# Which engine copies which PSUM tile, and in which PSUM unit a group lands: a spectral filter mix on one core

## The chip, the cores and the metric

The kernel runs on one core of a Trainium2 chip. A core has five engines that run their own instruction streams and meet at semaphores: TensorE (PE in the profile; its weight loads have a row of their own, PEld), VectorE (DVE), ScalarE (ACT), GpSimd (POOL) and SyncE (SP, used here to issue transfers). TensorE writes its results to PSUM, 8 banks of 512 float32 per partition; DVE and ACT copy them from there to SBUF. The metric is device time of the one core in microseconds, the median of several executions.

## The reference

Two global spectral filters, A and B, are applied to the same input `x` of 2048 by 1024 (bfloat16), and a gate per row mixes their results:

```python
X = rfft2(x)                       # over rows (2048) and columns (1024)
a = irfft2(X * (A_w_r + 1j * A_w_i))
b = irfft2(X * (B_w_r + 1j * B_w_i))
g = sigmoid((x * gate_w).sum(-1))  # one value per row
out = g * a + (1 - g) * b
```

The weights are 2048 by 513 each. `B_x` is not used.

## The kernel before, in words

There is no FFT instruction, so each Fourier transform is a chain of matrix products with constant tables. The 2048 rows are split as 32 times 64. The stages, in order:

- **Stage 1** (`stage1`): the 32-point transform along the rows, after DVE has folded the columns of `x` into sums and differences (`fold`).
- **Stage 2** (`stage2(i)`, 16 steps): the transform along the columns, two blocks of rows per step. 16 matmuls (L451, L460) write two banks: 0 and 1 for even `i`, 6 and 7 for odd. One copy, here called CS`i` (L466), brings the 128x1024 result to one of three buffers `CS` in SBUF, in bfloat16 and reordered.
- **Stage 4** (`stage4(i)`, 16 steps): the 64-point transform along the rows. Its matmuls (L477) read CS`i` and write banks 2 and 3 for even `i`, 3 and 4 for odd `i`, and banks 0 and 1 in the last step, 15. Bank 3, which two neighbouring steps share, is written by the second half of a step's matmuls. One copy, called X`i` (L485 on DVE or L487 on ACT), brings the result to one of eight buffers `X`. `swap(i)` then issues two transfers (L283) that exchange real and imaginary rows of X`i` into one of seven buffers `XS`; POOL's queue issues them up to step 8 and SP's queue from step 9 on.
- **Products** (`product`, L508, all on DVE): the spectrum, plain ("A") or swapped ("B"), times part 0 or 1 of both filters' weights. Results replace the weights in SBUF.
- **Stage 5** (`group`): the inverse 64-point transform, 32 groups of 8 columns each. A group is 16 matmuls (`group_mm`, L604) into one PSUM unit, a pair of banks (unit u is banks 2u and 2u+1), and one copy (`group_out`, L613 on DVE or L615 on ACT) out of it.
- **Stage 6** and **stage 7**: the inverse 32-point transform, in which the gate is mixed in through 16 tables (`rbgen`, L593, DVE), then the inverse transform along the columns and the final sums (L793, L829 on DVE, L834 on POOL) and stores.
- Beside these the row gate is computed from the spectrum: `gate_spectrum` (L522) after stage 2, `star_column` and `col0` for column 256, and `zsum` (L563, with the sigmoid copies L566) in stage 5.

The order of the work on each engine is the order of the calls to `P.add`; there is no planner. A dependence becomes a wait on a semaphore that counts the finished instructions of the other engine. Every engine works in its order, so an instruction that waits holds everything behind it. Around the change that order is:

- Steps 0 to 13 run `step(i)`: stage 4 of step i, X`i`, the swap, then stage 2 of step i+2 and CS`i+2`; after it gate sums, products from the list `ORDER[i]`, and in the first steps `save512` and the folds `fold3` that stage 2 will read later. So ACT copies X0, CS2, then CS3, X2, CS4, then CS5, X4, CS6, and so on; X1 and X3 are on DVE, in front of the products of their step.
- At the start of stage 5 a list `slots` says which unit comes next: `spare()` takes its first entry and puts it at the end. It begins as 3, 2, 1; unit 0 holds stage 4's step 15. Group 1 goes to unit 3, X15 is copied, group 2 goes to unit 2, the star column (a 32-wide result) to unit 1. Then unit 0 is put into the list at its end (L703): the order from there on is 3, 2, 1, 0. The groups that follow, 3, 4, 5, 6 and so on, take the units in this rotation. A group waits until the copy out of its unit is done.
- Groups run in the order 1 to 15, 0, then 16 to 31. All copies of groups are on ACT, but groups 20 and 27 (n of 4 and 11 in the loop at L722) and group 30 are on DVE. The 16 `rbgen` are issued on DVE right behind group 20's copy. Groups 30 and 31 are interleaved in two halves (`last_groups`).
- Stage 6 of row block 0 uses the unit that the rotation gives it by an assertion at L732; stage 7 uses fixed banks, `b0`, that alternate with the parity of r.

Of the kernel before, what the change touches and what calls it, by code (L numbers as in the profile page):

```python
# [5 lines left out]
ACT = mybir.ActivationFunctionType  # L6
# [226 lines left out]
def bass_gated_mix__spectral_gfnet__spectral_gfnet__prompt_kernel(nc, A_x, A_w_r, A_w_i, B_x, B_w_r, B_w_i, gate_w, out):  # L233
# [24 lines left out]
    def sl(t, off, dims, p0=0, np_=128, pstep=1):  # L258
        n = t.shape[1]
        return AP(t, p0 * n + off, [[n * pstep, np_]] + [list(x) for x in dims])  # L260

    def ps(col, dims):
        return AP(PS, col, [[4096, 128]] + [list(x) for x in dims])

    def bank(b):
        return ("ps", b)

    def fbo(kind, pm, m):
        return 128 * (4 * kind + 2 * pm + m)
# [6 lines left out]
    P = Prog()  # L276
# [18 lines left out]
    for _ in range(18):  # L295
        P.add("pe", lambda e: e.matmul(ps(7 * 512, [(1, 256)]), sl(CL, GRo, [(1, 128)]), sl(CL, GRo, [(1, 256)]), start=True, stop=True),
              r=["GRz"], w=[bank(7)])
# [124 lines left out]
    def fblock(cmb, j, t):  # L422
        if cmb in (1, 2):
            return sl(FT, cmb * 4096 + j * 2048 + t * 128, [(1, 128)])
        if t < 4:
            return sl(W, Eo(t // 2, cmb // 3, j) + t % 2 * RP, [(1, 128)])
        return sl(FT, cmb * 4096 + j * 2048 + (t - 4) * 128, [(1, 128)])

    def ekeys(i, cs, s):
        return [("E", i, cs, s)]  # L430
# [11 lines left out]
    def stage2(i, css=(0, 1), ab=(0, 1)):  # L442
        hf, p = SEQ[i]
        b0 = 6 * (i % 2)
        if 0 in ab:
            for cs in css:
                for t in (2 * p, 2 * p + 1):
                    for j in range(2):
                        o = ps((b0 + t % 2) * 512 + cs * 256 + 32, [(96, 2), (64, 2), (1, 32)])
                        rh = sl(F2, 256 + 512 * cs + 256 * j + hf * 128, [(1, 128)])  # L450
                        P.add("pe", lambda e, o=o, cs=cs, j=j, t=t, rh=rh: e.matmul(o, fblock(1 + cs, j, t), rh, start=(j == 0), stop=(j == 1)),  # L451
                              r=[("F1a" if p < 2 else "F1", cs, j), "F2"], w=[bank(b0 + t % 2)])
        if 1 in ab:
            for cs in css:
                for t in (2 * p, 2 * p + 1):
                    for w in range(2):
                        v = 1 - w if cs else w
                        o = ps((b0 + t % 2) * 512 + cs * 256 + 64 * v, [(224 - 128 * v, 2), (1, 32)])
                        rh = sl(F2, 1280 * cs + w * 128 + hf * 64, [(1, 64)])
                        op = P.add("pe", lambda e, o=o, cs=cs, t=t, w=w, rh=rh: e.matmul(o, fblock(3 * cs, w, t), rh, start=True, stop=True),  # L460
                                   r=ekeys(p, cs, w) + ["F2"], w=[bank(b0 + t % 2)])
        if css == (0,) or ab == (0,):
            return
        dst, src = sl(XF, CSo(i), [(1, 1024)]), ps(b0 * 512, [(128, 8), (1, 32), (32, 4)])
        kw = dict(r=[bank(b0), bank(b0 + 1)], w=[("CS", i % 3)], after=last1)
        P.add("act", lambda e: e.activation(dst, src, ACT.Copy), **kw)  # L466
        return op

    def stage4(i):
        bk = ((2, 3), (3, 4))[i % 2] if i < 15 else (0, 1)  # L470
        parts = [(1, 0, 1), (0, 1, 1)] if SEQ[i][1] == 0 else [(0, 0, 2)]
        for pm in (1, 0) if bk[0] == 3 else (0, 1):
            for kind, q, n in parts:
                for m in range(2):
                    o = ps(bk[pm] * 512 + q * 256, [(1, n * 256)])
                    rh = sl(XF, CSo(i) + 512 * q + 256 * m, [(512, n), (1, 256)])
                    P.add("pe", lambda e, o=o, kind=kind, pm=pm, m=m, rh=rh: e.matmul(o, sl(CK, fbo(kind, pm, m), [(1, 128)]), rh,  # L477
                                                                                      start=(m == 0), stop=(m == 1)),
                          r=[("CS", i % 3), "CK"], w=[bank(bk[pm])])

        def out():
            dst, src = sl(XF, Xo(i), [(1, 1024)]), ps(bk[0] * 512, [(256, 2), (512, 2), (1, 256)])
            kw = dict(r=[bank(k) for k in bk], w=[("X", Xk(i))], after=last1)
            if i in (1, 3):
                P.add("dve", lambda e: e.tensor_copy(dst, src), **kw)  # L485
            else:
                P.add("act", lambda e: e.activation(dst, src, ACT.Copy), **kw)  # L487

        return out

# [126 lines left out]
    def group(u, g, eng):  # L617
        group_mm(u, g, range(8), lambda q: q)
        group_out(u, g, eng, 0, 8, 1, 0, [("Z", 0), ("Z", 1)])
# [60 lines left out]
    slots = [3, 2, 1]  # L680

    def spare():
        slots.append(slots.pop(0))
        return slots[-1]
# [3 lines left out]
    def groups(n):  # L688
        for _ in range(n):
            group(spare(), todo.pop(0), "act")  # L690
# [9 lines left out]
    groups(1)  # L700
    star_column(2 * spare())
    dma("sp", "U5", sl(FT, U5o, [(2048, 8), (1, 1024)]).bitcast(u16), cst["U5"].ap().rearrange("p (a b) -> p a b", a=8), w=["U5"], after=[last2])
    slots.insert(3, 0)  # L703
    groups(8)
    for a in rest(10):
        product(*a)
# [15 lines left out]
    for n, g in enumerate(range(16, 32)):  # L722
        if n == 14:
            last_groups([spare(), spare()])
        elif n < 14:
            group(spare(), g, "dve" if n in (4, 11) else "act")
        if n == 1:
            zsum([spare(), spare()])
        if n == 4:
            for _ in range(16):  # L730
                rbgen(rb.pop(0), "dve")
    assert slots[-2:] == [0, 3], slots  # L732
    last5 = P.ops["pe"][-1]


# [1 line left out]
    Yo = lambda k, r: (8 * k + r // 2) * RP + 264 + r % 2 * 128  # L737
    OUT = [(MM, 1024 * k) for k in range(4)] + [(XF, 6144 + 1024 * k) for k in range(2)]

    S6B = lambda r: 4 if r % 2 else 6 if r else 2  # L740

    def stage6_mm(r, bs, pis):
        b0 = S6B(r)
        t6, o6, _ = RBS[r]
# [11 lines left out]
    def stage6(r):  # L756
        b0 = S6B(r)
        for k in range(2 if r == 0 else 1):
# [12 lines left out]
    def stage7(r):  # L771
        nonlocal pqc
        full, half = r in FULL, r in HALF
        b0 = 34 - 2 * r if r >= 14 else 2 * (r % 2)
        ot, oo = OUT[r % NOU]
        eo = 4096 + r % 2 * 1024
        es = sl(XF, eo, [(1, 1024)]).bitcast(f32)
# [20 lines left out]
        if full:  # L798
            for k in range(4):
                mm((b0 + 1) * 512, 0, 2, 1, k // 2, k % 2, k, 3)  # L800
            even(0, 512)
            for k0, n, bk in ((0, 2, b0),) if r < 15 else ((0, 1, b0), (1, 1, 0)):
                for k in range(4):
                    mm(bk * 512, k0, n, 0, k // 2, k % 2, k, 3)
                finals(k0, n, bk, XF, eo, [("EO", r % 2)])
        elif half:
            for e_ in (1, 0):
                for k in range(2):
                    mm((b0 + 1) * 512 + e_ * 256, 0, 1, 1, k, k ^ e_, k, 1)
            even(256, 256)  # L810
            for k in range(4):
                mm(b0 * 512, 0, 2, 0, k // 2, k % 2, k, 3)
            to = 4096 + (r % 2) * 1024
            for s, op in enumerate((ALU.add, ALU.subtract)):
                P.add("dve", lambda e, s=s, op=op: e.tensor_tensor(out=sl(MM, to + s * 512, [(1, 512)]).bitcast(f32),
                                                                   in0=ps((b0 + 1) * 512, [(1, 256)]), in1=es[:, :256], op=op),
                      r=[("EO", r % 2), bank(b0 + 1)], w=[("T", r % 2, s), ("XS", 4), ("XS", 5)])
            finals(0, 2, b0, MM, to, [("T", r % 2, 0), ("T", r % 2, 1)])
        else:
            for e_ in (1, 0):  # L820
                for ri in range(2):
                    for k in range(2):
                        mm((b0 + e_) * 512 + ri * 256, 0, 1, ri, k, k ^ e_, k, 1)
            even(0, 512)
            pk = pqc % NPQ
            pqc += 1
            pq = pk * 4096
            for s, op in enumerate((ALU.add, ALU.subtract)):
                P.add("dve", lambda e, s=s, op=op: e.tensor_tensor(out=sl(FT, pq + s * 2048, [(1, 1024)]).bitcast(f32), in0=ps(b0 * 512, [(1, 512)]),  # L829
                                                                   in1=es, op=op),  # L830
                      r=[("EO", r % 2), bank(b0)], w=[("PQ", pk, s)], after=[last5])
            pv = sl(FT, pq, [(2048, 2), (1, 1024)]).bitcast(f32).rearrange("p a (b c) -> p a b c", b=2)
            for s, op in enumerate((ALU.add, ALU.subtract)):
                P.add("pool", lambda e, s=s, op=op: e.tensor_tensor(out=ods(s, 0, 2), in0=pv[:, :, 0, :], in1=pv[:, :, 1, :], op=op),  # L834
                      r=[("PQ", pk, 0), ("PQ", pk, 1)], w=[("OU", r % NOU, s, k) for k in range(2)])
# [91 lines left out]
```

## Time and profile before

| | us |
|---|---|
| median of 3 runs | 119.57 (119.42 to 119.87) |
| the profiled execution | 119.76 |
| its span, first to last instruction | 117.6 |
| PE busy in the span | 110.5 |
| DVE busy | 101.4 |
| ACT busy | 97.5 |
| POOL busy | 33.8 |
| mean granted TensorE clock | 1.000 of full speed |

How to read it: all times inside the profile count from the span's first instruction; the 2.2 us between span and execution time lie around it. A row of the timeline gives the start, the duration, the engine, the source line (L485 is line 485 of the kernel), the operation, what it writes and reads, and, in brackets, how long its engine had been idle and what ended the idle time. Neighbouring instructions of one kind are merged into one row (x16). A row of the list of waits reads: engine, line, what it waited for, microseconds in total, how many times, the longest. The stages lie about here in the span: stage 1 up to 20.7, stages 2 and 4 from 20.8 to 51, stage 5 from 50.8 to 85.4, stages 6 and 7 from 85.3 to the end.

### The profile page before, as it was taken

The numbers are of one execution on the slowest core, as the hardware profiler recorded it, in microseconds if no ns is written. First come the engines' busy times: TensorE is split into PE (matmuls) and PEld (weight loads), VectorE is DVE, ScalarE is ACT, GpSimd is POOL, SyncE is SP. The second block draws the span as 40 slices with busy tenths as digits, with TensorE's granted clock in tenths as the row PEclk, the third lists the DMA queues.
The fourth block names the chain that finished last, engine by engine and source line by source line (L and its number), as shares of the span: only waits on it lengthen the run. The fifth ranks groups of instructions, "written<-read, shape, count | busy, mean of one in ns | idle before, by whom it ended". The sixth has DMA issues, their size and how long they took to land.

```text
span 117.6 us, 4242 instructions
## 1 busy us (share of the span) xinstructions
PE 110.5 (94%) x1812; PEld 88.5 (75%) x1812; DVE 101.4 (86%) x210; ACT 97.5 (83%) x117; POOL 33.8 (29%) x43
## 2 busy tenths in 40 slices
PE   6999999999999999997999999999989999999960
PEld 4566898875766757686999999999978777777530
DVE  0468998989999999999999999699569999899980
ACT  5239998988799999959999999997977889998620
POOL 1000030016655600000000000000003999999920
PEclk9999999999999999999999999999999999999999
DMA  3999999999999999963399800000000134426465
GB/s 72 303 416 417 416 358 353 354 347 351 370 361 359 368 363 363 361 230 137 84 342 398 298 6 0 6 0 6 0 6 3 66 147 155 178 95 224 154 243 188
DMA packets 17682, 26.14 MB, mean 222 GB/s; under 512 B 2112, under 2 KB 11072, under 8 KB 17664
## 3 DMA queue, kind: packets, MB, share of 16 engines
q1 hardware_dynamic: 16368, 23.00, 55.5%
q0 software_dynamic: 864, 2.36, 5.6%
q10 hardware_dynamic: 432, 0.52, 1.6%
q8 instruction: 14, 0.23, 0.8%
q14 instruction: 4, 0.03, 0.1%
HBM read 17.48 MB, written 4.19 MB: 184 GB/s over the span
## 4 chain that ended last, share of the span: by engine, by line
PE 79%; DMA 6%; ACT 4%; DVE 4%; SPq 2%; issue 2%; DVEq 0%
PE PS L604 25%; PE PS L782 15%; PE PS L477 12%; PE PS L379 9%; PE PS L753 6%; DMA W<-in_A_x_dram 6%; PE PS L451 6%; PE PS L460 3%; PE PS L522 2%; SPq L283 2%; ACT XF L487 2%; ACT W L615 1%; DVE XF L485 1%; DVE MM L793 1%; ACT XF L789 1%
## 5 line engine op out<-in xcount | busy, mean ns | idle before, releaser
L604 PE MATMUL PS<-CL,W 128*128 128x128 bf16 x512 | 32.2, 224 | 0.7 <-ACT W L615 0.6
L604 PEld LDWEIGHTS PS<-CL,W 128*128 128x128 bf16 x512 | 31.7, 145 | 1.1 <-ACT W L615 0.8
L834 POOL TENSOR_TENSOR MM<-FT 128x512 bf16<-128x512 f32 x14 | 17.5, 1297 | 48.9 <-DVE FT L829 48.9
L615 ACT ACTIVATE W<-PS 128x1024 bf16<-128x1024 f32 (+1 forms) x30 | 29.1, 1009 | 2.7 <-PE PS L604 2.6
L508 DVE TENSOR_TENSOR W<-XF,W 128x1024 bf16<-128x1024 bf16 (+1 forms) x38 | 22.4, 608 | 0.8 <-ACT XF L487 0.5
L508 DVE TENSOR_TENSOR W<-MM,W 128x1024 bf16<-128x1024 bf16 (+1 forms) x38 | 22.4, 613 | 0.4 <-DMA MM<-XF 0.2
L782 PE MATMUL PS<-FT,W 128*128 128x256 bf16 (+1 forms) x132 | 19.6, 299 | 0.2
L477 PE MATMUL PS<-XF,CK 128*128 128x512 bf16 (+1 forms) x72 | 17.9, 357 | 0.2 <-DVE XF L485 0.2
L766 ACT ACTIVATE W<-PS 128x1024 bf16<-128x1024 f32 (+1 forms) x15 | 14.8, 992 | 3.9 <-PE PS L753 3.9
L466 ACT ACTIVATE XF<-PS 128x1024 bf16<-128x1024 f32 x16 | 17.0, 1072 | 1.1 <-PE PS L460 1.0
L340 DVE TENSOR_TENSOR XF<-W 128x512 bf16<-128x512 bf16 (+2 forms) x34 | 11.4, 403 | 6.0 <-DMA W<-in_A_x_dram 5.8
L782 PEld LDWEIGHTS PS<-FT,W 128*128 128x128 bf16 x132 | 12.0, 98 | 5.4 <-DVE XF L793 0.7
L487 ACT ACTIVATE XF<-PS 128x1024 bf16<-128x1024 f32 x14 | 15.2, 1085 | 0.6 <-PE PS L477 0.6
L379 PE MATMUL PS<-MM,XF 128*128 128x256 bf16 x128 | 15.2, 276 | 0.5 <-DVE XF L340 0.3
L379 PEld LDWEIGHTS PS<-MM,XF 128*128 128x128 bf16 x128 | 12.3, 99 | 3.5 <-DVE XF L340 1.8
L390 ACT ACTIVATE FT<-PS 128x1024 bf16<-128x1024 f32 (+2 forms) x15 | 13.1, 1012 | 0.8 <-PE PS L379 0.8
L283 POOL DMA_DIRECT2D MM<-XF x18 | 9.9, 551 | 13.6 <-PE PS L477 8.0
L829 DVE TENSOR_TENSOR FT<-PS,XF 128x512 f32<-128x512 f32 x18 | 11.5, 684 | 0.5 <-ACT XF L789 0.2
L451 PEld LDWEIGHTS PS<-F,FT 128*128 128x128 bf16 x128 | 8.4, 98 | 3.1 <-ACT FT L390 0.2
L451 PE MATMUL PS<-F,FT 128*128 128x128 bf16 x128 | 10.2, 219 | 0.0
L789 ACT ACTIVATE XF<-PS 128x512 f32<-128x512 f32 (+1 forms) x16 | 8.5, 533 | 1.4 <-PE PS L782 1.4
L477 PEld LDWEIGHTS PS<-XF,CK 128*128 128x128 bf16 x72 | 4.7, 97 | 6.3 <-ACT XF L487 4.7
(62 smaller groups left out, 104.5 us busy)
## 6 DMA issues: line engine op xcount, KB each, us to landing
W<-in_A_x_dram SPq DMA_DIRECT2D x7, 512.0 KB, 7.5
out_dram<-MM SPq DMA_DIRECT2D x10, 256.0 KB, 2.3
MM<-XF POOLq DMA_DIRECT2D x18, 128.0 KB, 5.3
FT<-c_U SPq DMA_DIRECT2D x1, 2048.0 KB, 9.6
MM<-XF SPq DMA_DIRECT2D x14, 128.0 KB, 2.7
W<-in_A_w_r_dram SPq DMA_DIRECT2D x4, 256.5 KB, 6.4
W<-in_A_w_i_dram SPq DMA_DIRECT2D x4, 256.5 KB, 6.6
W<-in_B_w_r_dram SPq DMA_DIRECT2D x4, 256.5 KB, 6.9
```

Source lines behind the costliest of these rows:

```text
L379: P.add("pe", lambda e, o=o, lh=lh, rh=rh, s=s: e.matmul(o, lh, rh, start=(s == 0), stop=(s == 1)), r=[("xf", c % 2, q, h, s ^ j), ("M", c ...
L390: P.add("act", lambda e, s=src, d=dst: e.activation(d, s, ACT.Copy), **kw)
L451: P.add("pe", lambda e, o=o, cs=cs, j=j, t=t, rh=rh: e.matmul(o, fblock(1 + cs, j, t), rh, start=(j == 0), stop=(j == 1)), r=[("F1a" if p ...
L466: P.add("act", lambda e: e.activation(dst, src, ACT.Copy), **kw)
L477: P.add("pe", lambda e, o=o, kind=kind, pm=pm, m=m, rh=rh: e.matmul(o, sl(CK, fbo(kind, pm, m), [(1, 128)]), rh, start=(m == 0), stop=(m = ...
L487: P.add("act", lambda e: e.activation(dst, src, ACT.Copy), **kw)
L508: P.add("dve", lambda e: e.tensor_tensor(out=rows((1 - h) * 64 * RP + sw * HW), in0=sl(xt, xo + 128 * h + 64 * h0, [(0, 2), (256, 4 * ni), ...
L604: P.add("pe", lambda e, o=o, l0=l0, ab=ab: e.matmul(o, sl(W, HW * ab + l0, [(RP, 128)]), sl(CL, KIo[ab], [(1, 128)]), start=(ab == 0), sto ...
L615: P.add("act", lambda e: e.activation(dst, src, ACT.Copy), r=b, a=keys)
L766: P.add("act", lambda e, s=src, d=dst: e.activation(d, s, ACT.Copy), **kw)
L782: P.add("pe", lambda e: e.matmul(ps(col, [(1, n * 256)]), lh, rh, start=(k == 0), stop=(k == last)), r=[("Y", r), "DI"] + ["DJ"] * (full o ...
L834: P.add("pool", lambda e, s=s, op=op: e.tensor_tensor(out=ods(s, 0, 2), in0=pv[:, :, 0, :], in1=pv[:, :, 1, :], op=op), r=[("PQ", pk, 0), ...
```

## The change

Four edits, all of them on the order and placement of work; what is computed stays the same.

1. In stage 2 the copies CS3 and CS5 go from ACT to DVE; in stage 4 the copies X1 and X3 go from DVE to ACT.
2. Unit 0 is put into the rotation behind unit 3 in place of the end: the order becomes 3, 0, 2, 1. Group 4, the fourth of stage 5, lands in the unit that stage 4's step 15 used, group 5 in unit 2, group 6 in unit 1.
3. Group 19 is copied by DVE and group 20 by ACT (before, the other way round), and the 16 `rbgen` follow group 19's copy.
4. As the rotation ends differently, stage 6's row block 0 uses banks 0 and 1 (before 2 and 3), and stage 7's banks for even and odd r change places.

```diff
@@ stage2
-        P.add("act", lambda e: e.activation(dst, src, ACT.Copy), **kw)
+        if i in (3, 5):
+            P.add("dve", lambda e: e.tensor_copy(dst, src), **kw)
+        else:
+            P.add("act", lambda e: e.activation(dst, src, ACT.Copy), **kw)
@@ stage4
-            if i in (1, 3):
-                P.add("dve", lambda e: e.tensor_copy(dst, src), **kw)
-            else:
-                P.add("act", lambda e: e.activation(dst, src, ACT.Copy), **kw)
+            P.add("act", lambda e: e.activation(dst, src, ACT.Copy), **kw)
@@ start of stage 5
-    slots.insert(3, 0)
+    assert slots == [3, 2, 1]
+    slots.insert(1, 0)
     groups(8)
@@ second half of stage 5
-            group(spare(), g, "dve" if n in (4, 11) else "act")
+            group(spare(), g, "dve" if n in (3, 11) else "act")
         if n == 1:
             zsum([spare(), spare()])
-        if n == 4:
+        if n == 3:
             for _ in range(16):
                 rbgen(rb.pop(0), "dve")
-    assert slots[-2:] == [0, 3], slots
+    assert slots[-2:] == [1, 3], slots
@@ stage 6 and stage 7
-    S6B = lambda r: 4 if r % 2 else 6 if r else 2
+    S6B = lambda r: 4 if r % 2 else 6 * (r > 0)
...
-        b0 = 34 - 2 * r if r >= 14 else 2 * (r % 2)
+        b0 = 34 - 2 * r if r >= 14 else 2 - 2 * (r % 2)
...
-            for k0, n, bk in ((0, 2, b0),) if r < 15 else ((0, 1, b0), (1, 1, 0)):
+            for k0, n, bk in ((0, 2, b0),) if r < 15 else ((0, 1, b0), (1, 1, 2)):
```

## The prediction, made before the changed kernel was run

> **What bounds the kernel now.** I read the busy line and the chain of the page first, then the list of waits, then the timeline of the two places that the change touches. From the page and the list of waits:
>
> ```profile
> PE 110.5 (94%) x1812; PEld 88.5 (75%) x1812; DVE 101.4 (86%) x210; ACT 97.5 (83%) x117; POOL 33.8 (29%) x43
> PE 79%; DMA 6%; ACT 4%; DVE 4%; SPq 2%; issue 2%; DVEq 0%
> ...
> PEld PS L477 <- ACT XF L487: 4.7, 12, 0.5
> PEld PS L477 <- DVE XF L485: 1.2, 2, 0.7
> PEld PS L604 <- ACT W L615: 0.8, 1, 0.8
> ```
>
> PE carries 79% of the chain, so what counts is where PE stands still. In stages 2 to 4 it waits at L477 (stage 4's second pair of matmuls) for the copy of the step before, because two neighbouring steps share bank 3: 12 times behind ACT, twice behind DVE. In stage 5 the list holds one wait worth having, 0.8 us. Now the first steps of stage 4 (start, duration, engine, line; in brackets the idle time before and who ended it):
>
> ```profile
> 25.19 1.02 ACT L466 ACTIVATE XF<-PS 128x1024 bf16<-128x1024 f32 x1
> 26.00 1.23 DVE L485 CAST XF<-PS 128x1024 bf16<-128x1024 f32 x1
> 26.71 1.02 ACT L466 ACTIVATE XF<-PS 128x1024 bf16<-128x1024 f32 x1 [0.50 <-PE PS L460]
> 27.27 0.11 PEld L477 LDWEIGHTS PS<-XF,CK 128*128 128x128 bf16 x2 [0.70 <-DVE XF L485]
> 27.92 1.02 ACT L487 ACTIVATE XF<-PS 128x1024 bf16<-128x1024 f32 x1 [0.18 <-PE PS L477]
> 28.84 1.02 ACT L466 ACTIVATE XF<-PS 128x1024 bf16<-128x1024 f32 x1
> 29.65 1.22 DVE L485 CAST XF<-PS 128x1024 bf16<-128x1024 f32 x1
> 30.36 1.02 ACT L466 ACTIVATE XF<-PS 128x1024 bf16<-128x1024 f32 x1 [0.51 <-PE PS L460]
> 30.92 0.11 PEld L477 LDWEIGHTS PS<-XF,CK 128*128 128x128 bf16 x2 [0.50 <-DVE XF L485]
> 31.57 1.02 ACT L487 ACTIVATE XF<-PS 128x1024 bf16<-128x1024 f32 x1 [0.18 <-PE PS L477]
> ```
>
> L485 is stage 4's copy X1, then X3, on DVE (1.22 us); PE goes on 0.05 after each ends. L466 is stage 2's copy, here CS2, CS3, CS4, CS5. ACT idles 0.50, 0.18, 0.51 and 0.18 there. From X5 (33.39) on it never idles: 21 copies in 33.3 to 50.8, about 0.91 from start to start. So until X4 the loop PE-copy-PE sets the time; after it ACT does, and a shift of X4 is a shift of all of stage 4. Two ACT copies in a row start 0.92 apart (27.92, 28.84), before the first has ended. Then the start of stage 5 and its middle:
>
> ```profile
> 52.21 1.02 ACT L615 ACTIVATE W<-PS 128x1024 bf16<-128x1024 f32 x1 [1.20 <-PE PS L604]
> 53.13 1.02 ACT L487 ACTIVATE XF<-PS 128x1024 bf16<-128x1024 f32 x1
> 54.04 1.03 ACT L615 ACTIVATE W<-PS 128x1024 bf16<-128x1024 f32 x1
> 55.12 9.81 PEld L604 LDWEIGHTS PS<-CL,W 128*128 128x128 bf16 x160 [0.77 <-ACT W L615]
> ...
> 74.75 1.22 DVE L613 CAST W<-PS 128x1024 bf16<-128x1024 f32 x1 [1.08 <-PE PS L604]
> 75.89 2.77 DVE L593 TENSOR_TENSOR FT<-FT,XF 128x512 bf16<-128x512 bf16 x8
> ```
>
> ACT copies group 1, X15, group 2 in that order. PE's fourth group, at 55.12, waits for group 2's copy (ends 55.07), since it is put in group 2's unit. From there PE has no further gap until 85.4, at 9.81/10 = 0.98 a group. At 74.75 DVE, idle for 1.08, copies group 20.
>
> **Part 1: X1 and X3 to ACT, CS3 and CS5 to DVE.** Two copies go each way, so neither engine's sum changes; what changes is the queue each stands in.
> X1: its matmuls end at 25.96; ACT, busy with CS2 since 25.19, takes it at 25.19 + 0.92 = 26.11 and ends at 27.13, against 27.22 (the exact end on DVE): 0.09 earlier. PE's second pair, X2 and CS4 follow 0.09 earlier: X2 27.83, CS4 28.75. X3 is ready at 29.56, but ACT is free only at 28.75 + 0.92 = 29.67, so it ends at 30.70, against 30.87: 0.17. X4 starts 0.17 earlier (31.40), and CS6 0.92 behind it as now. Sum of part 1: -0.17. Bounds: steps 2 and 4 are 1.92 long (26.00 to 27.92, 29.65 to 31.57) and the steps between them 1.73, so at best 2 x 0.19 = -0.38; at worst ACT's two copies don't overlap, and the sum is +0.13 (first rival). I take -0.17, since the overlap stands in the rows.
> CS3 on DVE: its matmuls end at about 26.70, DVE has been free since 26.02, so it runs 26.73 to 27.95 (1.22, all seven 128x1024 casts from PSUM took 1.22). Stage 4's step 3 needs it at 28.28: covered by 0.3, and by 0.5 for CS5 (30.28 to 31.50, needed at 32.06). Beyond this cover a delay goes to PE one for one.
> Queued behind CS3 on DVE are a product, save512 and two folds; behind CS5 all other products. Product (1,A0) moves from 27.25 to about 27.87, the folds end at 30.2, CS5 holds until 31.5, and product (0,B0) comes at 32.64 instead of 32.36: DVE is **0.28 late**, 0.36 if nothing overlaps. From here to 73.67 it has no gap that could absorb it. Nearest rows for an upper end: were the whole first wait (26.02 to 26.71) to stay, 0.69. Who waits for DVE: group 1 needs the product at 49.80 (ends 50.24); it will want to start at 50.84 - 0.17 = 50.67, and 50.24 + 0.28 + 0.05 = 50.57, so 0.10 is left. Swap 14 on SP waits for DVE already (1.2 us, SP's own waits); it, swap 15, the star column's transfer and U5, DI, DJ behind it come up to 0.28 later, needed only at 58.9, 63 and 75. Swaps 1 and 3 on POOL issue 0.1 to 0.2 earlier, with POOL idle before them. Group 16 (67.6 when moved) needs products that end at 65.64 + 0.28, group 24 those at 73.95, 2 us ahead.
>
> **Part 2: group 4 in X15's unit.** Before, group 3 (53.29) would have let group 4 start at 53.29 + 0.98 = 54.27; it started at 55.12. After, it waits for X15's copy, in the moved times 52.96 + 1.02 + 0.05 = 54.03, while group 3 is done at 54.10. So the whole 0.86 goes, with 0.07 to spare. Next late: group 5 in unit 2 needs group 2's copy (54.90 + 0.05) at 55.08, 0.13 to spare; group 6 follows the star column's small copy, group 7 group 3's copy (55.9, wanted at 57.0). ACT starts copies 0.90 apart when it has a backlog, PE makes a group in 0.98, so its lag of 0.5 shrinks. Bounds: 0 and -0.86; I take -0.86.
>
> **Part 3: group 19 instead of 20 on DVE.** DVE's last product allows a start at 73.59 + 0.28 = 73.87; group 19 is done by PE at about 72.7 (20 at 73.7). DVE's idle 1.08 vanishes, the copy ends at 75.09 + 0.05. Its unit is wanted by group 23, sixth of the row of 14 from 71.54: 71.54 + 5 x 0.98 - 1.03 = 75.4. Cost 0, cover 0.25; without cover DVE's lateness lands on PE. The 16 table multiplications L593 follow at once and end about 0.9 earlier (80.5); group 27's copy, ready at 80.5, starts there. ACT has group 20 where it had 19, no later than now.
> **Part 4: new banks in stages 6 and 7.** Two units swap names; the first matmuls wait for group 31's half copy, which ends 0.7 after all copies of the banks in question. Cost 0, cover 0.7.
>
> **Sum.** -0.17 - 0.86 = -1.03, and nothing after 55.12 takes it back. The profiled execution took 119.76 (span 117.6, 2.2 around it) and becomes 118.73. It stands 0.19 above the median of 119.57, so the median becomes **118.54**.
>
> **Rivals.**
> *ACT's copies don't overlap.* X1 and X3 now follow CS2 and CS4 on the same engine. With 1.02 from start to start X3 ends at 31.0 instead of 30.87: part 1 is +0.13, the time 118.84. In stage 5 a copy would then take longer than PE's 0.98 per group and ACT would take back 0.04 in each of some 25 groups, 1.0 less the 0.2 to 0.3 that the units leave: about 119.6, no change. Against it: 0.92 and 0.90 in the rows above. The Trainium skill (Advanced Engine Details and Errata, section The Read-Write Bubble) says that ScalarE and VectorE show the memory latency as a bubble between two instructions. By that rule this rival would be the forecast; the trace's 0.92 between starts of 1.02 long copies does not agree. 0.08.
> *DVE's lateness reaches PE at group 1.* Price: lateness minus 0.38 (0.28 plus the 0.10 left). With 0.69 it is 0.31, the time 118.85. 0.10.
> *Slower: DVE becomes the bound.* Same place and price, lateness minus 0.38, one for one; every group behind is pushed. It eats the gain at 1.4 and is slower by 0.5% (0.60 us) from 2.0. For it: DVE has no gap between 32.4 and 73.7. Against: two waits of at most 0.7 don't add up to it, and the cast's price is the same in all seven rows. At 2.2 it gives 119.57 - 1.03 + 1.82 = 120.4. 0.05.
> *Part 1 does more.* The steps 2 and 4 shrink to 1.73: 118.33. 0.07, since X3 stands behind CS4.
> *It doesn't do what it says.* Group 4 would still wait for group 2. The semaphore counts ACT's copies in order and X15 comes before group 2, so I see no way; its 0.86 would leave 119.4. 0.02.
>
> **How the numbers follow.** Forecast 0.68, its own range 118.3 to 118.8 (0.2 for the spread of the three runs); rivals 0.08, 0.10, 0.05, 0.07, 0.02. A measurement of this kernel can tell about 0.5%, here 118.97. Faster: 0.68 + 0.10 + 0.07 and 0.02 of the first rival = 0.87; same 0.06 + 0.02 = 0.08; slower 0.05. The range 118.15 to 119.1 takes in the forecast, DVE's lateness up to 0.69, and the best case.
>
> **What would show it.** X1 and X3 as L487 on ACT; X4 near 31.4; a CAST of stage 2 on DVE near 26.7 and 30.3; group 4 directly behind group 3, no wait of L604 on L615 above 0.1; the CAST of stage 5 at 73.9 with no idle before it; group 18 on at 70.5 in place of 71.5. Wrong it would be if group 1 shows a wait for DVE, group 23 a wait for the cast, or ACT's copies in stage 5 end later and later behind PE's groups.

## The result, and the profile after

The changed kernel took 118.67 us in the median of 6 executions (118.47 to 119.08), the kernel before, run beside it, 119.80 in the median of its 6. The ratio is 0.9915, 95% interval 0.9891 to 0.9939: faster by 0.85%, clear of the interval. The prediction was a ratio of 118.54 / 119.57 = 0.9914. The profiled execution took 118.55 with a span of 116.3.

From the page of the profile and the list of waits of the changed kernel, where stage 4's matmuls are now line 480 and the casts of stage 2 line 467:

```profile
PE 109.9 (94%) x1812; PEld 88.4 (76%) x1812; DVE 101.1 (87%) x210; ACT 96.7 (83%) x117; POOL 33.8 (29%) x43
PE 81%; DMA 6%; ACT 5%; DVE 3%; SPq 2%; issue 1%; DVEq 0%
...
PEld PS L480 <- ACT XF L487: 5.7, 14, 0.6
```

All 14 waits of stage 4 are now behind ACT, and the line "PEld PS L604 <- ACT W L615: 0.8" is gone from the list. The timeline of stage 4's first steps, the rows that answer those of before (L469 on ACT is stage 2's copy, L487 stage 4's):

```profile
25.10 1.02 ACT L469 ACTIVATE XF<-PS 128x1024 bf16<-128x1024 f32 x1
26.00 1.03 ACT L487 ACTIVATE XF<-PS 128x1024 bf16<-128x1024 f32 x1
26.62 1.23 DVE L467 CAST XF<-PS 128x1024 bf16<-128x1024 f32 x1 [0.69 <-PE PS L460]
27.09 0.11 PEld L480 LDWEIGHTS PS<-XF,CK 128*128 128x128 bf16 x2 [0.61 <-ACT XF L487]
27.73 1.02 ACT L487 ACTIVATE XF<-PS 128x1024 bf16<-128x1024 f32 x1 [0.70 <-PE PS L480]
28.65 1.02 ACT L469 ACTIVATE XF<-PS 128x1024 bf16<-128x1024 f32 x1
29.56 1.03 ACT L487 ACTIVATE XF<-PS 128x1024 bf16<-128x1024 f32 x1
30.18 1.23 DVE L467 CAST XF<-PS 128x1024 bf16<-128x1024 f32 x1
30.64 0.11 PEld L480 LDWEIGHTS PS<-XF,CK 128*128 128x128 bf16 x2 [0.40 <-ACT XF L487]
31.29 1.02 ACT L487 ACTIVATE XF<-PS 128x1024 bf16<-128x1024 f32 x1 [0.70 <-PE PS L480]
```

The reader is to see two short waits of PE, 0.61 and 0.40, where there were 0.70 and 0.50, and the new wait of DVE, 0.69, in front of CS3. X0 began at 24.18 here and at 24.27 before, because the folds ahead of it wait for the input, which landed a little differently; times are best compared from X0 on. X4 comes 7.11 after X0, against 7.30. Then stage 5:

```profile
51.93 1.02 ACT L615 ACTIVATE W<-PS 128x1024 bf16<-128x1024 f32 x1 [1.20 <-PE PS L604]
52.85 1.02 ACT L487 ACTIVATE XF<-PS 128x1024 bf16<-128x1024 f32 x1
53.75 1.03 ACT L615 ACTIVATE W<-PS 128x1024 bf16<-128x1024 f32 x1
53.00 5.09 PEld L604 LDWEIGHTS PS<-CL,W 128*128 128x128 bf16 x82
...
73.78 1.22 DVE L613 CAST W<-PS 128x1024 bf16<-128x1024 f32 x1
74.91 2.76 DVE L593 TENSOR_TENSOR FT<-FT,XF 128x512 bf16<-128x512 bf16 x8
```

The weight loads of groups 3, 4, 5 and on are one row of 82 without a gap from 53.00, where the row used to end after 16. The cast at 73.78 has no bracket: DVE's idle 1.08 before it is gone.

The same marks from X0 on, in the two kernels and in two of the experiments below (us after the start of X0):

| | before | after | part 1 alone | part 2 alone |
|---|---|---|---|---|
| X4 starts | 7.30 | 7.11 | 7.11 | 7.30 |
| group 1 starts | 26.57 | 26.37 | 26.38 | 26.57 |
| group 4 starts | 30.85 | 29.80 | 30.69 | 30.02 |
| group 18 starts | 47.27 | 46.14 | 47.08 | 46.33 |
| end of the span | 93.28 | 92.16 | 93.09 | 92.38 |
| gain at the end | | 1.12 | 0.19 | 0.90 |

### The profile page after: what moved, and what is told of

It is laid out like the page before. It is cut to its first block, busy times and chain, and to the rows that moved or that the text cites. A ratio compares the mean times of both kernels' runs of the same rounds, so it can differ in the third digit from the quotient of the medians.

```text
span 116.3 us, 4239 instructions
## 1 busy us (share of the span) xinstructions
PE 109.9 (94%) x1812; PEld 88.4 (76%) x1812; DVE 101.1 (87%) x210; ACT 96.7 (83%) x117; POOL 33.8 (29%) x43
## 4 chain that ended last, share of the span: by engine, by line
PE 81%; DMA 6%; ACT 5%; DVE 3%; SPq 2%; issue 1%; DVEq 0%
PE PS L604 27%; PE PS L783 14%; PE PS L480 12%; PE PS L379 9%; PE PS L754 6%; DMA W<-in_A_x_dram 6%; PE PS L451 6%; PE PS L460 3%; PE PS L522 3%; SPq L283 2%; ACT XF L487 2%; ACT XF L790 1%; DVE MM L794 1%; PE PS L563 1%; ACT XF L469 1%
## 5 line engine op out<-in xcount | busy, mean ns | idle before, releaser
L604 PE MATMUL PS<-CL,W 128*128 128x128 bf16 x512 | 31.9, 225 | 0.0
L604 PEld LDWEIGHTS PS<-CL,W 128*128 128x128 bf16 x512 | 31.6, 145 | 0.3
L615 ACT ACTIVATE W<-PS 128x1024 bf16<-128x1024 f32 (+1 forms) x30 | 28.5, 1032 | 2.4 <-PE PS L604 2.3
L487 ACT ACTIVATE XF<-PS 128x1024 bf16<-128x1024 f32 x16 | 17.3, 1078 | 1.6 <-PE PS L480 1.4
L767 ACT ACTIVATE W<-PS 128x1024 bf16<-128x1024 f32 (+1 forms) x15 | 14.8, 992 | 3.9 <-PE PS L754 3.9
L469 ACT ACTIVATE XF<-PS 128x1024 bf16<-128x1024 f32 x14 | 15.0, 1079 | 0.1
```

Source lines behind the costliest of these rows:

```text
L604: P.add("pe", lambda e, o=o, l0=l0, ab=ab: e.matmul(o, sl(W, HW * ab + l0, [(RP, 128)]), sl(CL, KIo[ab], [(1, 128)]), start=(ab == 0), sto ...
L615: P.add("act", lambda e: e.activation(dst, src, ACT.Copy), r=b, a=keys)
L767: P.add("act", lambda e, s=src, d=dst: e.activation(d, s, ACT.Copy), **kw)
```

## Experiments: the parts one by one

**Part 1 alone.**

```diff
 # kernel before
+        if i in (3, 5): CS copy on "dve"   (stage2)
-        if i in (1, 3): X copy on "dve"    (stage4)
```

> Part 1 alone: CS3 and CS5 on VectorE, X1 and X3 on ScalarE, all else as before. Theory (two gains that add up, -0.17 and -0.86): X4 0.17 to 0.2 earlier counted from X0, group 4 still waits 0.8 for group 2's copy, time 0.2 under the kernel before, VectorE 0.28 late behind CS5. Rival (all of the gain is stage 5's, part 1 only moves the wait to another engine): no change, or up to 0.1 slower for VectorE's lateness.

Measured: ratio to the kernel before 0.9990 (0.9977 to 1.0002), about -0.12 us; here and below the interval follows in brackets. In the trace X4, group 1 and the end of the span come 0.19 earlier, as in the table, and group 4 waits 0.78 for group 2's copy. The trace bears the theory out; the times can't tell 0.19 from zero.

**Part 2 alone.**

```diff
 # kernel before
-    slots.insert(3, 0)
+    slots.insert(1, 0)
 # and the bank names of stages 6 and 7 as in the change
```

> Group 4 in unit 0 and the bank names that follow from it, nothing else: copies of stages 2 and 4 as before, group 20 on VectorE. Theory: group 4 starts 0.98 behind group 3, no wait of PE between 53 and 85, time 0.86 under the kernel before. Rival (the group 19 edit is needed, otherwise PE's saved time is taken back at VectorE's cast): a wait of PE for L613 near group 24, time only 0 to 0.4 under the kernel before.

Measured: 0.9920 (0.9904 to 0.9936), about -0.96 us. The weight loads around group 3 and 4 in its timeline:

```profile
53.23 0.21 PEld L527 LDWEIGHTS PS<-GSB,CK 128*128 128x128 bf16 x4
53.57 2.55 PEld L604 LDWEIGHTS PS<-CL,W 128*128 128x128 bf16 x41
```

No gap after 16 loads, no wait of PE for L613. So the group 19 edit isn't what makes part 2 pay.

**The change without part 3.**

```diff
 # changed kernel
-            group(spare(), g, "dve" if n in (3, 11) else "act")
+            group(spare(), g, "dve" if n in (4, 11) else "act")
 # and the 16 rbgen behind n == 4
```

> The changed kernel with group 20 in place of 19 on VectorE, as before. Theory: group 20 is done by PE at about the time (73.8) at which VectorE's products end, so the cast starts as early as group 19's did and nothing waits: time equal to the changed kernel within 0.1. Rival (part 3 pays): 0.2 to 0.5 slower than the changed kernel, with a wait of PE for the cast or for ScalarE.

Measured: 0.9911 (0.9897 to 0.9925), the changed kernel's 0.9915 within the intervals: part 3 is worth nothing that can be seen. Its profiled execution showed something else. DVE's and PE's rows in front of group 1 (the first two are products, the others weight loads of group 1):

```profile
48.22 0.44 DVE L508 TENSOR_TENSOR W<-MM,W 128x512 bf16<-128x512 bf16 x1
49.28 0.43 DVE L508 TENSOR_TENSOR W<-XF,W 128x512 bf16<-128x512 bf16 x1 [0.61 <-DMA W<-in_B_w_i_dram]
...
50.56 0.14 PEld L604 LDWEIGHTS PS<-CL,W 128*128 128x128 bf16 x1
51.04 1.97 PEld L604 LDWEIGHTS PS<-CL,W 128*128 128x128 bf16 x31 [0.33 <-DVE W L508]
```

DVE stands still for the last weights of filter B, which the first product of step 8 (the second row) needs; they landed at 49.18 in this execution (48.44 in that of the kernel before, 48.62 in that of the changed one). That product starts 0.1 after the landing, as it did in the changed kernel's profiled execution (48.71), so it is 0.57 late, and group 1's second weight load starts at 51.04 in place of 50.77. Group 1 thus pays 0.27 for it, and the end of the span comes 0.26 later from X0 on; the 0.33 in brackets is the idle time of PEld, not the delay. The two experiments on the loads below follow from this row.

**Group 4 in group 2's unit again.**

```diff
 # changed kernel
-    slots.insert(1, 0)
+    slots.insert(2, 0)
```

> The changed kernel with unit 0 put third into the rotation (3, 2, 0, 1): group 4 lands in group 2's unit again, group 5 in X15's. Theory (it is group 2's copy that holds group 4, not its place in the order): PE waits 0.77 before group 4 as before, time 0.86 above the changed kernel, that is 0.2 under the kernel before. Rival (what counts is that unit 0 is used early, fourth or fifth): time as the changed kernel.

Measured: 0.9987 (0.9977 to 0.9997), about -0.16 us, and the wait is back in the timeline:

```profile
53.03 1.05 PEld L604 LDWEIGHTS PS<-CL,W 128*128 128x128 bf16 x16
54.86 1.25 PEld L604 LDWEIGHTS PS<-CL,W 128*128 128x128 bf16 x19 [0.78 <-ACT W L615]
```

So it is group 2's copy that holds group 4; using unit 0 early is not enough. This kernel is parts 1 and 3 with another rotation, and its gain agrees with part 1 alone. The times of both (0.9990 and 0.9987) fit a part 1 of 0.1 to 0.2 us, though only the second is clear of 1.

## Experiments: how late DVE may be

**One idle reduction, about 0.6 us of DVE's time, behind CS5.**

```diff
 # changed kernel, step(3), ahead of products(3)
+        P.add("dve", lambda e: e.tensor_reduce(AT[:], sl(F2, 0, [(16, 32), (1, 16)]), ...), r=["F2"], w=["AT"])
```

> The changed kernel with one idle reduction of 0.7 us (128x512, as the one of line 539) on VectorE right behind CS5. Theory (VectorE's lateness reaches PE at group 1 beyond a cover of 0.08, read from the trace of the changed kernel: product ends 50.42, group 1 starts 50.55): group 1 waits 0.6 for VectorE, time 0.6 above the changed kernel. Rival (there is more cover, the last weights decide): 0 to 0.3 above.

Measured: 0.9942 (0.9922 to 0.9962), 0.3 us above the changed kernel's 0.9915, with intervals that overlap. The theory had 0.6; the time fits the rival's 0 to 0.3. The reduction lasts 0.68, and the next instruction starts 0.59 after the reduction's start. The profiled execution took longer than the median (119.90 against 119.05) and shows two places. The timeline of PE's weight loads, then one row of DVE:

```profile
50.62 0.14 PEld L604 LDWEIGHTS PS<-CL,W 128*128 128x128 bf16 x1 [0.23 <-DVE W L508]
51.10 1.95 PEld L604 LDWEIGHTS PS<-CL,W 128*128 128x128 bf16 x31 [0.33 <-DVE W L508]
...
76.61 1.53 PEld L604 LDWEIGHTS PS<-CL,W 128*128 128x128 bf16 x24 [1.01 <-DVE W L613]
```

```profile
60.61 0.29 DVE L555 TENSOR_TENSOR XF<-XST,W 128x64 bf16<-128x64 bf16 x2 [0.85 <-DMA XST<-XST]
```

At group 1 the last product that the group needs ends at 51.05, 0.63 later than in the changed kernel (50.42), and the second weight load, which is the first that needs it, starts at 51.10 against 50.77. So 0.30 of the lateness was covered and 0.33 was paid. Not all of the 0.63 need be the reduction's: the last weights landed at 49.24 in this execution, and the first product of step 8 started at 49.34, 0.1 behind them. Later DVE waits 0.85 for the star column's transfer: SP issued it at 56.93 in place of 55.55, and it landed at 60.52 in place of 57.96. SP was late because the issue of one transfer of swap 13, at 51.51, lasted 1.91 (0.52 in the changed kernel); why it did, no run shows, and SP's list of waits has none for a product of DVE there. Being now 1.6 late (its last product of all ends 51.30 after X0, against 49.68), DVE reaches the cast of group 19 too late for group 23, which waits 1.01. That second wait is in this execution; the median, 0.3 above the changed kernel, has room for the first alone. So the 1.01 is not shown to be the reduction's price.

**Three reductions.**

> The same with three reductions, 2.1 to 2.2 us. Theory of the prediction's slower rival (one for one from the cover on): 2.0 to 2.1 above the changed kernel, that is 1.0 above the kernel before: slower, ratio about 1.008. Rival (VectorE can catch up on the way, or PE's groups can wait elsewhere at no cost): under 1.5 above the changed kernel, not slower than before.

Measured: 1.0055 (1.0033 to 1.0076): slower than the kernel before, 1.7 us above the changed kernel, between the 2.0 to 2.1 of the theory and the rival's 1.5.

```profile
52.22 0.14 PEld L604 LDWEIGHTS PS<-CL,W 128*128 128x128 bf16 x1 [1.45 <-DVE W L508]
52.70 2.00 PEld L604 LDWEIGHTS PS<-CL,W 128*128 128x128 bf16 x31 [0.34 <-DVE W L508]
```

From X0 on the last product that group 1 needs ends 1.89 later than in the changed kernel and its second weight load starts 1.59 later: again 0.30 covered, the rest one for one. The end of the span is 1.72 later (93.88 from X0, against 92.16).

## Experiments: the last weights

**The constants CL and CV ahead of the last weights.**

```diff
 # changed kernel, order on SP's queue
-    weights of t 0 to 15, then CL, CV
+    weights of t 0 to 13, then CL, CV, then weights of t 14 and 15
```

> The changed kernel with the same transfers in another order: the loads of CL and CV (528 KB) stand ahead of the last eight weight loads in SP's queue. Theory (the last weights land, at 48.6, only just before the product that needs them, so a later landing goes to group 1 one for one): landing 1.4 later (528 KB at 360 GB/s), VectorE waits for the transfer by 1.3, group 1 and the end 1.2 to 1.4 later than in the changed kernel, about 119.9. Rival (the weights have room): time as the changed kernel.

Measured: 1.0001 (0.9980 to 1.0022): all of the gain is gone, about 1.0 us, from the order of 528 KB.

```profile
50.15 0.43 DVE L508 TENSOR_TENSOR W<-XF,W 128x512 bf16<-128x512 bf16 x1 [1.50 <-DMA W<-in_B_w_i_dram]
...
51.91 1.97 PEld L604 LDWEIGHTS PS<-CL,W 128*128 128x128 bf16 x31 [0.33 <-DVE W L508]
```

DVE waits 1.50, the second load of group 1 starts at 51.91 against 50.77: 1.14 later, a little less than expected, since 0.30 of DVE's 1.44 (50.15 against 48.71) is covered at group 1 as above. So the weights have no room of their own.

**Fewer weights, in three kernels.**

```diff
 # changed kernel; kernel before; part 1 alone
+                if key == 3 and f:      # filter B, t 8 to 11
+                    memset on POOL in place of the loads
```

These kernels leave out a part of filter B's output.

> The changed kernel without four of the weight loads (filter B's rows of t 8 to 11, 1 MB; the rows are set to zero on GpSimd instead, so B's part of the output is incomplete). Theory: the last weights land 2 to 3 us earlier, VectorE never waits for them, and what is left is VectorE's own lateness: time 0 to 0.3 under the changed kernel, X and group rows as there. Rival (the weights bound stages 2 to 4 by themselves): 0.5 to 2 under.

> The kernel before without the same four weight loads (B's rows of t 8 to 11 set to zero, B's part of the output incomplete). Theory: its products were not held by the weights in the profiled execution (last landing 48.44, product at 48.53), but are in others: time 0 to 0.4 under the kernel before. What counts is the distance to the changed kernel made light in the same way: 0.19 + 0.90 = 1.1, ratio of the two about 0.991.

> Part 1 alone (CS3, CS5 on VectorE, X1, X3 on ScalarE), light in the same way. Theory (part 1 is worth the 0.19 seen in the trace, and late weights hide some of it in many executions): 0.19 under the light kernel before, more than the 0.12 that part 1 alone gave with all weights. Rival (part 1 is worth less than its trace): 0.1 or less under the light kernel before.

Measured, against the kernel before with all loads: changed kernel made light 0.9881 (0.9858 to 0.9905), kernel before made light 0.9966 (0.9952 to 0.9981), part 1 made light 0.9937 (0.9913 to 0.9961). 1 MB less to load thus gives the kernel before 0.4 us, clear of its interval, and the changed kernel 0.4 us as well, though there the two intervals overlap. That is more than the theory's 0 to 0.3 for the changed kernel and less than the rival's 0.5.

But this 0.4 us does not lie in front of group 1, nor anywhere else inside the span. The record has the span of every execution. For the kernel before it is 117.63 in the mean light and 117.62 with all loads; for the changed kernel 116.50 light and 116.52 with all loads. What shrank is the time around the span, 2.2 us with all loads and 1.8 in all three light kernels. Why it shrank, no run shows. The marks from X0 of the light changed kernel say the same: they are those of the changed kernel (group 1 26.38, end 92.16). What the last weights do inside the span is seen in DVE's steps, here the last product of step 7 and the first of step 8, in the changed kernel and then in the light one (there L512 is the product), whose last weights had landed at 46.39:

```profile
48.22 0.44 DVE L508 TENSOR_TENSOR W<-MM,W 128x512 bf16<-128x512 bf16 x1
48.71 0.42 DVE L508 TENSOR_TENSOR W<-XF,W 128x512 bf16<-128x512 bf16 x1
...
48.41 0.44 DVE L512 TENSOR_TENSOR W<-MM,W 128x512 bf16<-128x512 bf16 x1
48.76 0.42 DVE L512 TENSOR_TENSOR W<-XF,W 128x512 bf16<-128x512 bf16 x1
```

From start to start it is 0.49 in the changed kernel and 0.35 in the light one; it is 0.35 too in part 1 alone, with all loads, where the last weights had landed at 48.23 (48.40, 48.75), and 0.45 in the kernel before (48.08, 48.53). So the last weights held DVE for 0.14 and 0.10 in these two executions, with no bracket in the row. The cover of 0.30 at group 1 takes in the 0.14, so it cost PE nothing there; a later landing is paid, as the 0.27 and the 1.14 above show.

The distance between the light kernels is 0.9881 / 0.9966 = 0.9915, the same as with all weights. Part 1's is 0.9937 / 0.9966 = 0.9971, 0.35 us, but the two intervals overlap, and the trace of the light part 1 ends 93.10 after X0, 0.18 earlier than the kernel before: whether late weights hide some of part 1 stays open.

## Why the prediction was right, point by point

- **Part 1, -0.17.** The trace gives -0.19 at X4 and at every later mark. The steps came as worked out: X1 0.10 later in its start but earlier in its end, X3 0.91 behind CS4, DVE's wait of 0.69 in front of CS3. The time of part 1 alone does not tell this from zero; the marks do. One count in the working was off: from X5 to 50.8 ACT makes 19 such copies, not 21, which changes no term.
- **ACT's copies overlap.** X3 started 0.91 after CS4 (28.65, 29.56) although a copy lasts 1.02. The Trainium skill (Advanced Engine Details and Errata, section The Read-Write Bubble) says that on ScalarE memory latency shows as a bubble between instructions; these rows show none from one copy's end to the next one's start, since the next copy starts before the first one's end. The rival that has the copies 1.02 apart is out.
- **Part 2, -0.86.** Group 4 follows group 3 by 0.98 in place of 1.83. From X0 on part 2 alone gains 0.83 by group 4 and 0.94 by group 18; the 0.1 more on the way I have not traced.
- **Part 3 and part 4, nothing.** Right: the change without part 3 is as fast, and stage 6 waits 0.39 for ACT's copy before and after. With part 3 the cast ended at 74.99, 0.2 ahead of group 23 (75.23), where 0.25 had been worked out.
- **DVE 0.28 late.** The last product of all ends 49.68 after X0, against 49.40: 0.28. That it fits so well is in part luck: the product (0,B0), where the 0.28 was worked out, starts 0.25 later from X0 on (32.52 against 32.36), and the rest is about what the last weights add, which held DVE for 0.14 in one execution and 0.10 in the other. The price, one for one, was right too, and so was the slower rival as a mechanism: the three reductions made the kernel slower at group 1.
- **The cover at group 1 was mis-sized.** I had 0.10 left of 0.38, taking the group's first weight load as the one that needs the last product. It is the second, 0.22 later; the two runs with reductions show 0.30 left, and so do the late landings (0.57 late, 0.27 paid; 1.44 late, 1.14 paid). The slower rival therefore decides from a lateness of about 2.2, not 2.0.
- **Missing: the weights.** The prediction named what waits for DVE but not what DVE waits for at 48.5. I read "no gap" on DVE as DVE's own bound; but a wait of 0.10 to 0.14 for a transfer is in both kernels, shown by the step from start to start and not by a gap. It did not falsify the number because it is about the same in both and group 1's cover takes it in; that a landing as late as in the change without part 3 takes 0.27 of the gain was not in the working.

The median stands 0.13 above the forecast of 118.54, and the kernel before stood 0.23 above its earlier median in the same comparison; as a ratio the forecast was within 0.0001. The interval of the ratio is 0.0024 to either side, so that closeness is luck; what the runs bear out is the two terms, each at its own mark.

## What to carry to other kernels

When several PSUM units rotate, follow each unit's last reader in the order of the copying engine: a unit whose copy is queued one place earlier was worth 0.85 us here, nearly a whole copy, at no cost that a run shows. Before making an engine later or earlier, look on both sides of the first thing that depends on it: the exact instruction that waits, and the transfer that lands just ahead of it. A wait of 0.1 us for such a transfer left no gap in these profiles, so the steps from start to start are to be compared with those of a run in which the transfer landed early. When an edit leaves work out, compare the spans as well as the times: here the 0.4 us lay outside the span. A swap of work between two engines with equal sums is priced by the queues: what stands in front of the moved instruction, and what stands behind it.

## What was not expected of the hardware

The last of the weight loads landed between 48.2 and 49.2 us in the profiled executions of six kernels with the same loads in the same order, a spread of 1 us, while the start of X4 and of group 1, counted from X0, agreed within 0.02 us for equal code. The start of X0 itself moved between 24.14 and 24.52, with the landing of the input. Differences of 0.2 us are thus better read from a mark inside the trace than from the whole time.
